# Moving bonus products, a bonus shuffle and two weight differences in a fused RWKV6 + SiLU kernel

## The chip, the cores and the metric

The kernel runs on one core of a Trainium2 chip. Its time is the device time of a launch in microseconds (us), given as the median of several runs. A profiled execution is one launch recorded by the hardware profiler; its span runs from the first to the last recorded instruction and is a little shorter than the launch's own time. The engines are TensorE (PE in the profile; its weight loads are PEld), VectorE (DVE), ScalarE (ACT), GpSimd (POOL) and SyncE (SP, which here issues the DMAs).

## The reference

All data are float32. Batch 4, 8 heads, 768 tokens, head dimension 48; then a two-layer network over the 3072 tokens.

```python
# rwkv6: r, k, v, w are (4, 8, 768, 48), u is (8, 48)
for t in range(S):
    kt, vt, rt, wt = k[:, :, t], v[:, :, t], r[:, :, t], w[:, :, t]
    cur = einsum('bhd,bhe->bhde', u * kt, vt)
    y[:, :, t] = einsum('bhd,bhde->bhe', rt, state + cur)
    state = wt[..., None] * state + einsum('bhd,bhe->bhde', kt, vt)
x = y.transpose(0, 2, 1, 3).reshape(3072, 384)
h = x @ w_in                        # 384 x 2048
out = (h * sigmoid(h)) @ w_out      # 2048 x 384
```

## The kernel before, in words

**Units.** The work is cut into 12 units: six chunks of 128 tokens, each for two pairs of batches. Unit i covers 2 batches x 8 heads x 128 tokens. Instead of stepping through tokens, a unit builds for each head a 128 x 128 matrix `score` of token against token, by levels: level l joins blocks of c = 2^l tokens. `score_products` (L687 on, its matmuls recorded as L698 or L706) makes a level's entries on TensorE, and they are copied under a mask into `score` (L716 for a whole level, L803 for a corner of one, or ACT copies at L796 where c is 32 or more). `grow_queries` (DVE, L621), `grow_keys` (POOL, L639) and `prepare` (DVE, L774) multiply the decays into queries and keys between levels. From unit 2 on two levels are made together: `burst(i, l)` makes levels l and l + 1. Then `y_values` multiplies `score` by the values, `update` moves the state on (L882 to L898), and the result goes to `xt`, the input of the network.

**Bonus.** The diagonal of `score` is the "bonus" r·(u k), and near neighbours are made with it. Units 0 and 1 do it for pairs of tokens on TensorE's side; units 2 and 3 for pairs of tokens on POOL and DVE:

- `load_rk(i)` has SP load r and k of the unit into `tokens_rk` (four transfers, L107).
- `bonus(i, x)` has three POOL products: x = 0 at L442, x = 1 at L444, x = 2 at L446 (times u).
- `bonus_sum(i, x)` has DVE reduce the products into `own_sums` (L451; two at L455), and behind the last of them four SP transfers bring the sums to their rows (`diag`).
- `bonus_spread(i)` has five ACT copies into `both_b` and a DVE shuffle (L589 to L592), and `bonus_write(i)` has two masked DVE copies into `score` (L598).

From unit 4 on the same is done for blocks of 8 tokens (`block_bonus` L501, `block_sum` L535, `block_move`, `block_spread` with ACT copies at L562/L564 and a shuffle at L565, `block_write` at L571). Unit 4 is NPAIR, unit 2 is NTOK; NL is 7 and FIRST is 3.

**The network.** `up(i, m)` makes two of the sixteen slices of h (L990, then the SiLU into `gt` on ACT, L999). For unit 0 `down` (L1012) multiplies plainly by `w_out_sb`. From unit 1 on the second product is made by seven products of half size (`quarter`, L1056) from sums and differences: `sums` on the gt side (DVE, L1038), `weight_sums` on the weight side (DVE, L1030, once for the whole kernel, four steps 0 to 3 that write into `own` and `w_out_sb`). The results are added up at L1065 (DVE).

**The weights.** w_in and w_out arrive in 16 pieces, loaded by SP (L206), and each is rounded before TensorE reads it: `head_weight` (ACT, L223 and L225), `tail_weight` (ACT, L231), `join_weight` (two DVE operations, L242 and L243), `add_weight` (POOL, L255), which writes `w_in_sb`, `w_out_sb` or `own`. Pieces 8 and later belong to w_out.

**The order.** It is written out by hand. `do(...)` calls the steps one by one, and each step puts its instructions at the end of its engines' streams; nothing reorders them later. An engine takes its stream strictly in that order. The first units have long `do` lists of their own; from unit 3 on `mix(i)` gives a list of groups for unit i, and `room` says how many steps of the network (of units i - 1 and i - 2) follow each group. Semaphores between engines are set by the framework from reads and writes of the tiles.

Around the change, the order before is: the scores of unit 1's last level, weight piece 8, `y` and `update` of unit 1, piece 9, then pieces 10 to 15 each with a few steps of `up`, `down` and of unit 2 (`others`), then unit 2's levels 2 to 6.

Of the kernel before, what the change touches and what calls it, by code (L numbers as in the profile page):

```python
# [8 lines left out]
F32 = mybir.dt.float32  # L9
# [29 lines left out]
def kernel(  # L39
# [11 lines left out]
    nc = tc.nc  # L51
# [3 lines left out]
    L = 128  # L55
# [378 lines left out]
    def bonus(i, x):  # L434


        engine = nc.gpsimd if i > 0 or x == 0 else nc.vector
        if x == 0:
            ruk[i] = tokens_rk[:, 1] if i < NTOK else pt.tile([128, H, 2, D], F32, name="ruk", bufs=1)

            ruk[i, 0] = tokens_rk[:, 0, :, 0] if i < NTOK else ruk[i][:, :, 0]
            engine.tensor_tensor(out=ruk[i, 0], in0=rk(i, 0)[:, :, 1], in1=rk(i, 1)[:, :, 0], op=ALU.mult)  # L442
        elif x == 1:
            engine.tensor_tensor(out=ruk[i], in0=rk(i, 0), in1=rk(i, 1), op=ALU.mult)  # L444
        else:
            engine.tensor_tensor(out=ruk[i], in0=ruk[i], in1=u_bc[:, :, None, :].to_broadcast([128, H, 2, D]), op=ALU.mult)  # L446
# [229 lines left out]
    def corner(l, x):  # L676

        return x % 2, x if x % 2 == 0 else (L >> l) - 1 - x
# [2 lines left out]

    def score_products(i, l, queries, sc):
        c, ni = 1 << l, L >> (l + 1)
        if i > 0 or l == NL - 1:
            for p in range(NP):
                for x in range(4 if c == 32 else 2):
                    for e in range(2):  # L687
                        rows = slice(PD * e, PD * e + D)
                        if c >= 32:
                            b, first = corner(l, x)  # L690
                            q = (p, 2 * NP - 1 - p)[b]
                            to, have = sc[e][x * c:(x + 1) * c, q, first // 2 * c:(first // 2 + 1) * c], queries[rows, q, (first + 1) * c:(first + 2) * c]
                        else:
                            apart = 2 * (NP - p) - 1
                            to = dims_of(sc[e][x * 64:(x + 1) * 64, p, :], 32 * x, [apart * L // 2 + 32 - 64 * x, 2], [1, 32])
                            have = dims_of(queries[rows, p, :], 64 * x + c, [apart * L + 64 - 128 * x, 2], [2 * c, 32 // c], [1, c])
                        m = 32 if c == 32 else 64
                        nc.tensor.matmul(to, lhsT=tk[i][rows, X[l % 2] + p, x * m:(x + 1) * m], rhs=have, start=True, stop=True)  # L698
            return

        for p in range(NP):
            for e in range(2):
                rows = slice(PD * e, PD * e + D)

                apart, r_p, s_p = 2 * (NP - p) - 1, queries[rows, p, :], sc[e][:, p, :]
                nc.tensor.matmul(bass.AP(tensor=s_p.tensor, offset=s_p.offset,  # L706
                                         ap=[s_p.ap[0], [apart * L // 2, 2], [1, L // 2]]),
                                 lhsT=tk[i][rows, X[l % 2] + p, :],
                                 rhs=bass.AP(tensor=r_p.tensor, offset=r_p.offset + c,
                                             ap=[r_p.ap[0], [apart * L, 2], [2 * c, ni], [1, c]]),  # L710
                                 start=True, stop=True)
# [75 lines left out]
    def keep_level(i, l):  # L787
        c = 1 << l
        for e in range(2):
            if c < 32 and (i > NTOK or l == FIRST):  # L790
                keep_masked(i, l, e, made[i, l])
                continue
            for x in range(4 if c == 32 else 2):
                if c >= 32:
                    b, first = corner(l, x)
                    nc.scalar.copy(  # L796
                        out=score[x * c:(x + 1) * c, i % NSC, e, b * NP:(b + 1) * NP, (first + 1) * c:(first + 2) * c],
                        in_=made[i, l][e][x * c:(x + 1) * c, b * NP:(b + 1) * NP, first // 2 * c:(first // 2 + 1) * c])
                    continue
                rows = slice(x * 64, (x + 1) * 64)  # L800
                for b in range(NB):
                    half, inner = (x, 1 - x)[b], [1, c]
                    nc.vector.copy_predicated(  # L803
                        out=dims_of(score[rows, i % NSC, e, b * NP, :], 64 * half + c, [L, NP], [2 * c, 32 // c], inner),
                        mask=dims_of(masks[l][rows, b], 32 * half, [0, NP], [c, 32 // c], inner),
                        data=dims_of(made[i, l][e][rows, b * NP, :], 32 * half, [L // 2, NP], [c, 32 // c], inner))

    def go_on(i, l):

# [118 lines left out]
    def mix(i):  # L928
# [15 lines left out]
        def start(j):  # L944
            return [*[(product, j, l) for l in range(1, NL)], (grow_own, j, 1)]

        end = [[*at(ahead, *bonus_steps(i + 1, 0, 1, 2, 3))],
               [*at(i < len(units) - NB, (turn_apart, i), (turn_k, i)), *at(ahead, *turns(i + 1))],
               [(y_state, i), *both(y_values, i), *both(update, i), *at(ahead, *start(i + 1)),
                *at(ahead, *sum_steps(i + 1, 0, 1), *bonus_steps(i + 1, 4, 5)), (move_x, i)]]  # L950
        if i < NPAIR:
            groups = [[*both(turn, i, "w"), (product, i, 0)],
                      [*both(turn, i, "k"), *both(turn, i, "r"), (odd_ones, i)], [(start_levels, i), (prepare_keys, i, 1)],
                      [(prepare, i, 1), *[(product, i, l) for l in range(1, NL)]],
                      [(burst, i, 1), (keep_level, i, 1)],
                      [(keep_level, i, 2), (go_on, i, 2)],
                      [(prepare, i, 3), (reverse_v, i), (bonus, i, 0)],
                      [(burst, i, 3), (keep_level, i, 3), (bonus_sum, i, 0), (bonus, i, 1), (bonus, i, 2)],
                      [(keep_level, i, 4), (go_on, i, 4), (bonus_sum, i, 1), (load_rk, i + 1), (load_u,)],
                      [(prepare, i, 5), (make_block_mask,), (bonus_spread, i), (bonus_write, i)],  # L960
                      [(burst, i, 5), (keep_level, i, 5), (keep_level, i, 6), (go_on, i, 6)], *end]
        else:
            groups = [[], [(odd_keys, i, 2), (grow_keys, i, 2, False), (grow_queries, i, 2), *sum_steps(i, 2)],
                      [(prepare, i, 3), *bonus_steps(i, 6, 7)],
                      [(burst, i, 3), (keep_level, i, 3), *sum_steps(i, 3, 4), (block_move, i), *at(ahead, (load_rk, i + 1))],
                      [(keep_level, i, 4), (go_on, i, 4)],
                      [(prepare, i, 5), (reverse_v, i)],
                      [(block_spread, i), (block_write, i)],
                      [(burst, i, 5), (keep_level, i, 5), (keep_level, i, 6), (go_on, i, 6)], *end]

        loads = block_loads(i + NSLOT) if i + NSLOT < len(units) else []
# [153 lines left out]
    for m in range(1, 4):  # L1125
# [1 line left out]
    do((head_weight, 8), (join_weight, 7), (scores, 1, 5), (grow_keys, 1, 6), (add_weight,), (tail_weight, 8), (up, 0, 6),  # L1127
       (bonus_write, 1))

    do((scores, 1, NL - 1), (join_weight, 8), (add_weight,), (up, 0, 7), *both(y, 1), (turn_apart, 1),  # L1130
       (tail_weight, 9), (turn_k, 1), (dense_x, 1, 0), (head_weight, 9, [0]), (dense_x, 1, 1), (head_weight, 9, [1]),
       (join_weight, 9), (add_weight,), (tail_weight, 10), (head_weight, 10), *both(update, 1), (up, 1, 0), *both(turn, 2, "w"))
    blocks = block_loads(3)

    others = {0: [(up, 1, 1), (down, 0, 0, 0), *both(turn, 2, "k"), (product, 2, 0), (product, 2, 1)],
# [4 lines left out]
    for m in range(6):  # L1140
# [2 lines left out]
    second.append(ctx.enter_context(tc.tile_pool(name="po", bufs=1, space=bass.MemoryType.PSUM)))  # L1143

    blocks = block_loads(4)
    do(*blocks[0:2], (level, 2, 2), (prepare, 2, 3), (weight_sums, 1), (down, 0, 1, 0), (down, 0, 0, 3), (down, 0, 1, 1),
       (sums, 1, 0), (bonus, 2, 0), (bonus_sum, 2, 0))
    do(blocks[2], (burst, 2, 3), (keep_level, 2, 3), (keep_level, 2, 4), (go_on, 2, 4), (prepare, 2, 5), (bonus, 2, 1),
       (bonus, 2, 2), (down, 0, 1, 2), (bonus_sum, 2, 1), (load_rk, 3), (sums, 1, 1), *blocks[3:7], (down, 0, 1, 3))
    do((burst, 2, 5), (keep_level, 2, 5), (keep_level, 2, 6), (go_on, 2, 6), (up, 1, 6), (bonus_spread, 2), (bonus_write, 2),  # L1150
       (load_values, 3), (turn_apart, 2), (turn_k, 2), (up, 1, 7), (sums, 1, 2))
    do((sums, 1, 3), (y_state, 2), *both(y_values, 2), *both(update, 2),
       (move_x, 2),
       *blocks[7:])
# [1 line left out]
    for i in range(3, len(units)):  # L1156
        steps = downs(i - 2) + ups(i - 1)
        groups = mix(i)
        if i == NTOK + 1:

            groups[2].append((weight_sums, 2))
            groups[4].insert(1, (weight_sums, 3))
        room = (1, 1, 0, 2, 1, 1, 1, 1, 1, 2, 2, 1, 1, 0) if i < NPAIR else (3, 2, 2, 1, 1, 1, 2, 1, 1, 1, 0)
        for group, count in zip(groups, room):
            do(*group)
            for step in steps[:count]:
                do(*step)
            steps = steps[count:]
# [32 lines left out]
```

## Time and profile before

| what | value |
|---|---|
| median of 3 runs | 612.73 us (612.69 to 615.25) |
| profiled execution, its own time | 611.3 us |
| span of the profiled execution | 609.5 us, granted TensorE clock 0.997 |
| PE busy | 594.1 us, 97% of the span |
| DVE, POOL, ACT busy | 423.8, 367.2, 232.7 us (70%, 60%, 38%) |
| L990 (first product of the network), 1152 matmuls | 258.9 us, 382 ns each |
| L255 `add_weight` | 1.82 us each |
| L242 and L243 `join_weight` | 0.96 and 0.95 us |
| L442, L444, L446 bonus products of a pair unit | 1.18, 1.81, 1.80 us |
| L1030 `weight_sums` | 1.75 and 2.22 us |
| unit 2: burst of levels 1, 3, 5 starts at | 88.59, 105.74, 113.82 us |

Times in the timeline are microseconds from the start of the span. A row of the timeline gives the start, the duration, the engine, the line, the operation with its output and inputs, and how many instructions were put together; behind it in brackets stands the idle time of the engine ahead of that row and what ended it. A wait that is given to an engine is the one that ended last by the profile.

### The profile page before, as it was taken

The page shows a single profiled execution, that of the slowest core. Times are in us where ns is not written, and L with a number is a line of the kernel's source. Part 1 is how long each engine was busy: PE and PEld are TensorE (multiplying, and loading weights), DVE is VectorE, ACT ScalarE, POOL GpSimd, SP SyncE. Part 2 cuts the span into 40 slices and gives each one's busy share as a digit, 9 for nine tenths or more (in the row PEclk, how much of TensorE's full clock was granted, in tenths as well). Part 3 has the DMA queues.
Part 4 walks back from the last instruction along what each step waited for, and adds up shares of the span by engine and source line. Part 5 has one row for each costly group of instructions (what it writes and reads, how often), then busy time and mean ns, then how long its engine had stood idle before and what let it go on. Part 6 is the DMA issues. An engine that isn't in the chain of part 4 may idle for free.

```text
span 609.5 us, 15190 instructions
## 1 busy us (share of the span) xinstructions
PE 594.1 (97%) x5998; PEld 530.7 (87%) x5998; DVE 423.8 (70%) x715; ACT 232.7 (38%) x516; POOL 367.2 (60%) x414
## 2 busy tenths in 40 slices
PE   8999999899999997999999999999999999999997
PEld 7778876699889897889889889989989989989997
DVE  7879779898795495587588587487587597561041
ACT  6799792431530440351351252242252242241110
POOL 6998488557667278378468578568568658500000
PEclk9999999999999998999999999999999999999999
DMA  9966774353543643643543552552452312100000
GB/s 222 300 164 169 147 232 49 72 98 48 128 62 53 135 61 53 129 65 52 121 70 53 113 80 51 108 89 50 97 95 48 81 44 53 36 3 27 26 1 26
DMA packets 203079, 53.44 MB, mean 88 GB/s; under 512 B 186752, under 2 KB 194816, under 8 KB 203008
## 3 DMA queue, kind: packets, MB, share of 16 engines
q1 hardware_dynamic: 201424, 51.88, 41.6%
q8 instruction: 47, 0.77, 0.6%
q10 hardware_dynamic: 1584, 0.59, 0.4%
q14 instruction: 24, 0.20, 0.1%
HBM read 43.21 MB, written 5.24 MB: 79 GB/s over the span
## 4 chain that ended last, share of the span: by engine, by line
PE 72%; DVE 12%; DMA 4%; POOL 3%; ACT 3%; issue 3%; SPq 3%; DVEq 0%; POOLq 0%; ACTq 0%
PE p_h L990 31%; PE p_o L1056 30%; PE p_m L855 2%; DVE score L716 2%; DVE temps L1038 2%; DVE tr L621 2%; SPq L123 2%; PE p_sc L698 2%; POOL tk L639 2%; PE p_m L698 1%; DMA raw<-in_w_dram 1%; PE p_m L847 1%; DMA tokens_w<-in_w_dram 1%; DVE p_w L242 1%; DMA raw<-in_r_dram 1%
## 5 line engine op out<-in xcount | busy, mean ns | idle before, releaser
L990 PE MATMUL p_h<-xt,w_in_sb 128*128 128x256 f32 x1152 | 258.9, 382 | 1.8 <-POOL w_in_sb L255 1.1
L990 PEld LDWEIGHTS p_h<-xt,w_in_sb 128*128 128x128 f32 x1152 | 215.9, 190 | 32.8 <-POOL w_in_sb L255 1.2
L999 ACT ACTIVATE gt<-p_h 128x512 f32<-128x512 f32 x90 | 53.3, 596 | 189.2 <-PE p_h L990 188.8
L639 POOL TENSOR_TENSOR tk<-tk,tw 128x256 f32<-128x256 f32 x128 | 93.7, 753 | 43.5 <-issue 22.9
L1056 PE MATMUL p_o<-own,temps 128*128 128x192 f32 x528 | 90.2, 331 | 4.5 <-DVE temps L1065 4.5
L1056 PEld LDWEIGHTS p_o<-own,temps 128*128 128x128 f32 x528 | 87.6, 193 | 5.4 <-DVE temps L1065 5.3
L1056 PE MATMUL p_o<-w_out_sb,gt 128*128 128x192 f32 x508 | 87.4, 328 | 0.0
L1056 PEld LDWEIGHTS p_o<-w_out_sb,gt 128*128 128x128 f32 x508 | 82.7, 190 | 0.9 <-issue 0.4
L501 POOL TENSOR_TENSOR ruk<-tokens_rk 128x768 f32<-128x768 f32 (+1 forms) x32 | 50.0, 1573 | 52.0 <-DMA tokens_rk<-in_k_dram 31.9
L1038 DVE TENSOR_TENSOR temps<-gt 128x256 f32<-128x256 f32 x84 | 56.9, 677 | 22.4 <-ACT gt L999 22.4
L621 DVE TENSOR_TENSOR tr<-tr,tw 128x512 f32<-128x512 f32 x61 | 56.4, 924 | 15.3 <-PE p_m L698 12.4
L422 POOL TENSOR_TENSOR tw<-tw 128x256 f32<-128x256 f32 (+6 forms) x83 | 43.3, 521 | 36.4 <-DVE tw L374 32.5
L609 ACT COPY tk<-tk 128x256 f32<-128x256 f32 x52 | 20.9, 403 | 99.0 <-POOL tk L639 71.7
L1065 DVE TENSOR_TENSOR partial<-p_o,partial 128x192 f32<-128x192 f32 x33 | 11.8, 358 | 38.9 <-PE p_o L1056 38.7
L1038 DVE TENSOR_TENSOR temps<-temps,gt 128x256 f32<-128x256 f32 x43 | 32.1, 748 | 1.5
L716 DVE COPY_PREDICATED score<-mask,p_sc 128x512 f32<-128x512 int8 x42 | 31.1, 795 | 2.7 <-PE p_sc L698 2.5
L1056 PE MATMUL p_o<-w_out_sb,temps 128*128 128x192 f32 x176 | 30.4, 326 | 0.0
L1065 DVE TENSOR_TENSOR temps<-p_o,partial 128x192 f32<-128x192 f32 x22 | 7.9, 357 | 31.9 <-PE p_o L1056 22.4
L860 ACT COPY yt<-p_m 48x512 f32<-48x512 f32 x40 | 23.2, 581 | 14.9 <-PE p_m L855 8.7
L1056 PEld LDWEIGHTS p_o<-w_out_sb,temps 128*128 128x128 f32 x176 | 28.9, 190 | 0.0
L698 PEld LDWEIGHTS p_sc<-tr,tk 48*32 48x32 f32 (+1 forms) x1312 | 18.1, 119 | 11.6 <-issue 6.3
L501 POOL TENSOR_TENSOR spare<-tokens_rk 128x384 f32<-128x384 f32 (+1 forms) x16 | 28.1, 1754 | 0.0
(180 smaller groups left out, 845.7 us busy)
## 6 DMA issues: line engine op xcount, KB each, us to landing
w_out_sb<-in_moe_w_in_dram SPq DMA_DIRECT2D x6, 768.0 KB, 7.5
w_out_sb<-in_moe_w_out_dram SPq DMA_DIRECT2D x4, 768.0 KB, 5.2
own<-in_moe_w_out_dram SPq DMA_DIRECT2D x4, 768.0 KB, 5.9
tokens_rk<-in_r_dram SPq DMA_DIRECT2D x8, 384.0 KB, 4.4
tokens_rk<-in_k_dram SPq DMA_DIRECT2D x8, 384.0 KB, 5.3
tokens_w<-in_w_dram SPq DMA_DIRECT2D x8, 384.0 KB, 6.5
xt<-yt SPq DMA_DIRECT2D x60, 48.0 KB, 2.0
raw<-in_w_dram SPq DMA_DIRECT2D x80, 32.0 KB, 2.4
```

The source lines that it names most:

```text
L422: engine.tensor_tensor(out=up, in0=t[:, :, 0::2], in1=t[:, :, 1::2], op=ALU.mult)
L501: mul = lambda out, one, two: nc.gpsimd.tensor_tensor(out=out, in0=one, in1=two, op=ALU.mult)
L609: nc.scalar.copy(out=keys(i, X[(l + 1) % 2] * L + c, [4 * c, blocks], [c, 2], [1, c]), in_=keys(i, NP * L + c, [4 * c, blocks], [NP * L + ...
L621: nc.vector.tensor_tensor(out=odd, in0=odd, in1=tw[i][l][:, :, 0::2][:, :, :, None].to_broadcast([128, Q, L >> (l + 1), c]), op=ALU.mult)
L639: nc.gpsimd.tensor_tensor(out=out, in0=have, in1=odd_products(i, l, b, *blocks), op=ALU.mult)
L698: nc.tensor.matmul(to, lhsT=tk[i][rows, X[l % 2] + p, x * m:(x + 1) * m], rhs=have, start=True, stop=True)
L716: nc.vector.copy_predicated(out=dst, mask=masks[l][:, :, None].to_broadcast([128, NB, NP, ni, c]), data=sc[e].rearrange("p (b q) (i c) -> ...
L860: nc.scalar.copy(out=yt[i][PD * e:PD * e + D, :, b, :], in_=p_yt[i, e][PD * b:PD * b + D])
L990: nc.tensor.matmul(p_h[:, a, :], lhsT=w_in_sb[:, c, f * 128:(f + 1) * 128], rhs=xt[i][:, c, :], start=(c == 0), stop=(c == KC - 1))
L999: nc.scalar.activation(out=gt[i, m], in_=p_h, func=AF.Silu)
L1038: nc.vector.tensor_tensor(out=out, in0=one, in1=two, op=op)
L1056: nc.tensor.matmul(p, lhsT=left(f), rhs=right[:, f, :], start=(f == 0), stop=(f == FH - 1))
```

## The change

Five edits, all in the order of the steps or in the form of one step:

1. Unit 2's three bonus products and their sums are issued right behind the scores of unit 1's last level, among weight pieces 8 and 9, instead of among unit 2's own levels 2 to 5. Their results go into the tiles `spare` and `partial` instead of a tile `ruk`. The load of unit 3's r and k goes with them.
2. `bonus_spread(2)` is issued ahead of unit 2's burst of levels 5 and 6, and `bonus_write(2)` ahead of `up(1, 6)`.
3. `weight_sums(1)` and `weight_sums(2)` are issued behind unit 2's burst of levels 5 and 6 (before: ahead of `down(0, 1, 0)`, and in unit 3's third group).
4. Unit 2's level 4 uses the full form of `score_products` and of the masked copy, as level 3 does.
5. Unit 4's `block_spread` and `block_write` are issued behind its levels 5 and 6 instead of ahead of them.

```diff
         if x == 0:
-            ruk[i] = tokens_rk[:, 1] if i < NTOK else pt.tile([128, H, 2, D], F32, name="ruk", bufs=1)
+            if i == NTOK:
+                free = pt.tile([128, 4, DM // 2], F32, name="partial", bufs=1)
+                ruk[i] = free.rearrange("p x d -> p (x d)").rearrange("p (h s d) -> p h s d", h=H, s=2)
+            else:
+                ruk[i] = tokens_rk[:, 1] if i < NTOK else pt.tile([128, H, 2, D], F32, name="ruk", bufs=1)
...
+            if i == NTOK:
+                ruk[i, 0] = spare[:, 0:H * D].rearrange("p (h d) -> p h d", h=H)
...
-        if i > 0 or l == NL - 1:
+        if (i > 0 or l == NL - 1) and (i, l) != (NTOK, FIRST + 1):
...
-            if c < 32 and (i > NTOK or l == FIRST):
+            if c < 32:
                 keep_masked(i, l, e, made[i, l])
                 continue
...
-        end = [[*at(ahead, *bonus_steps(i + 1, 0, 1, 2, 3))],
+        end = [[*at(i == NPAIR, (block_spread, i), (block_write, i)), *at(ahead, *bonus_steps(i + 1, 0, 1, 2, 3))],
...
-                      [(block_spread, i), (block_write, i)],
+                      [*at(i > NPAIR, (block_spread, i), (block_write, i))],
...
-    do((scores, 1, NL - 1), (join_weight, 8), (add_weight,), (up, 0, 7), *both(y, 1), (turn_apart, 1),
+    do((scores, 1, NL - 1), (bonus, 2, 0), (bonus, 2, 1), (join_weight, 8), (add_weight,), (bonus_sum, 2, 0), (bonus, 2, 2), (up, 0, 7), *both(y, 1), (turn_apart, 1),
        (tail_weight, 9), (turn_k, 1), (dense_x, 1, 0), (head_weight, 9, [0]), (dense_x, 1, 1), (head_weight, 9, [1]),
-       (join_weight, 9), (add_weight,), (tail_weight, 10), (head_weight, 10), *both(update, 1), (up, 1, 0), *both(turn, 2, "w"))
+       (join_weight, 9), (add_weight,), (tail_weight, 10), (head_weight, 10), *both(update, 1), (bonus_sum, 2, 1), (load_rk, 3), (up, 1, 0), *both(turn, 2, "w"))
...
-    do(*blocks[0:2], (level, 2, 2), (prepare, 2, 3), (weight_sums, 1), (down, 0, 1, 0), (down, 0, 0, 3), (down, 0, 1, 1),
-       (sums, 1, 0), (bonus, 2, 0), (bonus_sum, 2, 0))
-    do(blocks[2], (burst, 2, 3), (keep_level, 2, 3), (keep_level, 2, 4), (go_on, 2, 4), (prepare, 2, 5), (bonus, 2, 1),
-       (bonus, 2, 2), (down, 0, 1, 2), (bonus_sum, 2, 1), (load_rk, 3), (sums, 1, 1), *blocks[3:7], (down, 0, 1, 3))
-    do((burst, 2, 5), (keep_level, 2, 5), (keep_level, 2, 6), (go_on, 2, 6), (up, 1, 6), (bonus_spread, 2), (bonus_write, 2),
-       (load_values, 3), (turn_apart, 2), (turn_k, 2), (up, 1, 7), (sums, 1, 2))
+    do(*blocks[0:2], (level, 2, 2), (prepare, 2, 3), (down, 0, 1, 0), (down, 0, 0, 3), (down, 0, 1, 1), (sums, 1, 0))
+    do(blocks[2], (burst, 2, 3), (keep_level, 2, 3), (keep_level, 2, 4), (go_on, 2, 4), (prepare, 2, 5), (down, 0, 1, 2),
+       (bonus_spread, 2), (sums, 1, 1), *blocks[3:7], (down, 0, 1, 3))
+    do((burst, 2, 5), (keep_level, 2, 5), (keep_level, 2, 6), (go_on, 2, 6), (bonus_write, 2), (up, 1, 6), (weight_sums, 1),
+       (load_values, 3), (turn_apart, 2), (turn_k, 2), (up, 1, 7), (weight_sums, 2), (sums, 1, 2))
...
-            groups[2].append((weight_sums, 2))
```

More of the change, by code (lines that the diff above doesn't have):

```diff
@@ L789, in keep_level @@
         for e in range(2):
-            if c < 32 and (i > NTOK or l == FIRST):
+            if c < 32:
                 keep_masked(i, l, e, made[i, l])
                 continue
[L793 to L806, printed above, removed]
+            for x in range(L // c):
+                b, first = corner(l, x)
+                nc.scalar.copy(
+                    out=score[x * c:(x + 1) * c, i % NSC, e, b * NP:(b + 1) * NP, (first + 1) * c:(first + 2) * c],
+                    in_=made[i, l][e][x * c:(x + 1) * c, b * NP:(b + 1) * NP, first // 2 * c:(first // 2 + 1) * c])
     def go_on(i, l):
```

## The prediction

> **What bounds the kernel now.** I read the page first: engines, the chain that ended last, TensorE's waits. Then I went through the two stretches that the change touches (60 to 140 us, 200 to 240 us) engine by engine. The chain, and the complete list of TensorE's waits for other engines between 60 and 240 us (columns: engine, tile, line, releaser; us in total, times, longest):
>
> ```profile
> PE 72%; DVE 12%; DMA 4%; POOL 3%; ACT 3%; issue 3%; SPq 3%; DVEq 0%; POOLq 0%; ACTq 0%
> ```
> ```profile
> PE p_o L1056 <- DVE temps L1065: 4.5, 2, 3.3
> PE p_sc L698 <- DVE tr L621: 1.6, 1, 1.6
> PE p_h L990 <- POOL w_in_sb L255: 1.1, 1, 1.1
> PE p_m L698 <- POOL tk L639: 0.9, 1, 0.9
> PE p_o L698 <- DVE tr L774: 0.3, 1, 0.3
> ```
>
> TensorE is the bound: 97% busy, and here it waits 8.4 us in all. Work that the change takes from DVE, POOL or ACT pays only through one of these rows; work that it makes late costs as soon as TensorE needs the result. From 65 to 110 us TensorE is busy 5.00 of every 5.00 us, so there is no pause to absorb a delay.
>
> TensorE's timeline (start, duration, count, idle before and releaser) places what matters:
>
> ```profile
> 78.16 2.74 PE L1012 MATMUL p_m<-w_out_sb,own 128*128 128x384 f32 x8
> ...
> 88.59 0.70 PE L698 MATMUL p_sc<-tr,tk 48*64 48x64 f32 x32
> ...
> 113.82 0.75 PE L698 MATMUL p_sc<-tr,tk 48*32 48x32 f32 x64 [1.56 <-DVE tr L621]
> ...
> 137.54 0.69 PE L698 MATMUL p_m<-tr,tk 48*64 48x64 f32 x32 [0.95 <-POOL tk L639]
> ...
> 183.41 5.47 PE L1056 MATMUL p_o<-own,temps 128*128 128x192 f32 x32 [1.22 <-DVE temps L1065]
> ...
> 233.43 7.15 PE L1056 MATMUL p_o<-own,temps 128*128 128x192 f32 x32 [3.33 <-DVE temps L1065]
> ```
>
> At 78.16 the first down product of unit 0 starts on w_out_sb. 88.59 is burst(2,1), 113.82 burst(2,5), 137.54 burst(3,2). The next two views decide the forecast: SP's DMAs, then POOL's instructions, around the place where unit 2's bonus products are to go.
>
> ```profile
> 66.93 1.30 SPq L107 DMA_DIRECT2D tokens_rk<-in_r_dram  x2
> 68.33 1.27 SPq L107 DMA_DIRECT2D tokens_rk<-in_k_dram  x2
> ```
> ```profile
> DMA to landing us min/median/max: 6.4/6.4/6.6
> ```
> ```profile
> 67.30 1.81 POOL L255 TENSOR_TENSOR w_out_sb<-temps 128x768 uint32<-128x768 uint32 x1 [3.52 <-issue]
> 73.52 1.83 POOL L255 TENSOR_TENSOR w_out_sb<-temps 128x768 uint32<-128x768 uint32 x1 [4.41 <-ACT temps L225]
> 77.69 1.82 POOL L255 TENSOR_TENSOR w_out_sb<-temps 128x768 uint32<-128x768 uint32 x1 [2.34 <-ACT temps L223]
> ```
>
> Unit 2's r and k are issued between 66.9 and 69.6; the last starts at 69.0 and lands 6.4 us later, at **75.4**. The POOL rows are add_weight for pieces 8, 9, 10. Pieces 8 and 9 end at 69.1 and 75.35, only 9.1 and 2.8 us before the matmuls at 78.16 need them.
>
> **What the Trainium skill says.** "Perfetto Trace Analysis", "DMA Instruction — HWDGE (DVE, Sync)": the profiled DMA row ends when the sequencer is done; the data movement comes later. The trace agrees: 0.6 us per issue, 6.4 us to landing. "TensorE: Matmul & The Clock Gate", architectural detail: ACT, DVE and GpSimd queues are strict FIFO. So an instruction that waits at the head holds all behind it; no row before disagrees. Same page, "What's actually happening": an idle window of about 3.4 us halves the clock. After the 3.33 us gap at 233, 32 matmuls take 7.15 us, 5.47 in the row of 183: agrees, worth 1.7 us. "SBUF — State Buffer", "SBUF: two separate sides": a DVE operation with two SBUF inputs and a GpSimd one exclude each other. L1038 takes 0.42 us alone and 1.92 or 2.03 while POOL works: agrees.
>
> **Part 1, bonus products of unit 2.** Before, POOL's three (1.18, 1.81, 1.80 us) and DVE's three sums (3 x 0.54) ran at 105 to 115 us. Now POOL's order is add 7, bonus 0, bonus 1, add 8, bonus 2, add 9; DVE's is join 8, sum, join 9, state copies, two sums, transposes, join 10. All wait in order for the landing at 75.4.
> POOL: bonus 0 ends 76.65, bonus 1 78.5, add 8 80.3 (was 69.1), bonus 2 82.15, add 9 84.0 (was 75.35). TensorE reaches the down product at 78.16: it waits 2.2 us for piece 8, runs two matmuls, waits 2.4 us for piece 9. That alone is 4.6 us.
> DVE: sum 77.25, join 9 79.25 (a pair takes 2.0), state copies 80.4, two sums behind bonus 2 83.25, transposes of w 84.5, join 10 86.5 where it was 77.5. The weight chain goes on from there, each step behind the one before on its engine: add 10 (1.82) 88.35; on DVE a transpose pair (1.3) and join 11 (2.0) 89.75, on POOL two L422 (1.73) and add 11 91.95; transposes and join 12 93.0, five L422 (2.06) and add 12 95.8; unit 2's start_keys (L663, 1.30) 97.1. TensorE, already 4.6 late, meets them in order: up(1,2) 85.4 to 88.1, 0.3 us for piece 10, 2.3 for piece 11, and 1.45 ahead of burst(2,1), since start_keys stands behind add 12. The sum 4.6 + 0.3 + 2.3 + 1.45 is **+8.7 us**: burst(2,1) near 97.3, not 88.59. The floor is 4.6, if the chain of 10 to 12 catches up. Behind it TensorE is full again: burst(2,2) near 105.9, burst(2,3) near 114.4.
> SP: four diag transfers and the four issues of load_rk(3), some 0.6 us each, move ahead of the `own` loads of pieces 14 and 15 (77.62); they wait for the sums at 83.25, so those loads go out near 88 and land 5.9 later, about 94. Piece 14 was joined at 89.94 and will be near 98: nothing. load_rk(3) waits for bonus 2 (82.15), which frees its room; its reader comes after 130: nothing. The rooms `spare` and `partial` have no other user until up(1,3) and unit 1's quarters: nothing.
>
> **Part 2, what leaves the stages of 97 to 121 us.** Ahead of burst(2,5) DVE loses weight_sums(1) (2.22), the first sum (0.54), 8 corner copies (2.03) for 2 full ones (2 x 0.65), and contention in the 2.32 us L621 (1.0 alone): 4.8 us, against a gap of 1.56: **-1.56**. What would be late next is L774, 0.3, also behind the same chain. The full form on TensorE takes 1.16 us instead of 0.69: **+0.45**. ACT's both_b copies no longer wait for diag (DVE idles 2.26 us at 118.3 for them), off TensorE's path: 0, between 0 and -0.3.
>
> **Part 3, weight_sums 1 and 2** go to DVE behind burst(2,5); their users are unit 1's quarters, from 138 us, at least 15 us later: 0. From ahead of burst(3,2), 2.2 us and its lock against POOL disappear: the gap 0.95 goes, **-0.95** (none, if POOL's L639 is late for itself).
>
> **Part 4, unit 4's shuffle** goes behind level 6. DVE no longer idles 8.03 us for ACT's `spare` (at 209.13), so the sums start after L621. But L621 itself waits for the burst of level 6, which ends at 209.55: of the 2.65 us of shuffle and L571, 2.2 are won there. Then the shuffle waits in order on ACT, whose copies now stand behind 12 score copies and a silu: 214.65; two L571 (2.5) end 217.45, the last sums 219.9, the next transposes start as before (219.95 for 220.03). The gaps of 183 and 233 stay: **0**, between -6.25 (3.33 + 1.22 + 1.7 of clock) and +2.5, should the copies lie later.
>
> Sum: 8.7 - 1.56 + 0.45 - 0.95 = +6.6 on the profiled 611.3 (span 609.5): 617.9. The median of the runs, 612.73, lies 1.4 above; I take 612.73 + 6.3, **619.0**, since the catch-up of pieces 10 to 12 is likelier partial than nil.
>
> **Rivals.** (A) *Faster.* The wait on unit 2's loads isn't felt and the clock drop at 233 goes: -1.56 - 0.95 + 0.45 - 3.33 - 1.7 = -7.1, 605.6; with the gap of 183 too, 604.4. It decides at the landing: add 9 ends landing + 8.5, and TensorE needs it at 79.5, so r and k must be there by 71.0. For it: add 8 alone would have 9 us of slack. Against: the landing is 75.4 and SP's queue ahead of it is unchanged. Chance 0.07. (B) *Near no change.* The delay stands, but unit 4's move removes both gaps and the clock drop: +6.6 - 6.25, about 613.1. Against: the place of the copies on ACT. Chance 0.06. (C) *Slower still.* The new gaps between 78 and 97 us, 4.6 us idle within 6, lower the clock: +1.7 to +3.4, 621 to 622.5. For: 3.33 us sufficed at 233; against: two pieces with matmuls between. Chance 0.18. (D) *Catch-up.* Only the floor: +4.6 - 2.06 = +2.5, 615.2, inside what a measurement can tell. For: the durations of the chain are those of rows that overlapped other work; against: every link above is in order on one engine. Chance 0.09. My forecast has the remaining 0.60.
>
> **How the numbers follow.** Low end 614.5 takes in D; high end 622.5 takes in C; A and B are left out, 0.13, and some of the ends. About 0.5% (3.06 us) is what a measurement of this kernel can tell from no change: faster is under 609.7 (A, 0.07), within it B and D (0.15), slower over 615.8 my forecast and C (0.78).
>
> **What would show it.** Right: bonus 0 on POOL shows some 9 to 12 us of idle time released by DMA tokens_rk, TensorE's down product at 78 waits for POOL w_out_sb (L255) over 4 us, burst(2,1) starts near 97.3, no gap ahead of burst(2,5), the gaps of 183 and 233 still there some 7 us later. Wrong: r and k land before 71; burst(2,1) under 92; or no clock below 0.9 between 235 and 250.

## The result and the profile after

The changed kernel takes **618.93 us** (median of 6 runs, 617.5 to 621.25) where the kernel before takes 612.5 (6 runs, 610.88 to 615.25). The ratio is 1.012, with a 95% interval of 1.0095 to 1.0145: slower by some 6 to 9 us. The forecast was 619.0. The profiled execution took 619.96 us, its span is 618.2 us. One execution each of E1 and E6 took twice the usual time and one of E7 was more than 1.5% above that kernel's fastest; the medians and ratios below leave these three out.

The lines of the changed kernel are 6 higher than before for the steps from the bonus products to `prepare` (L448 is L442, L627 is L621, L704 is L698) and 3 lower from `turn_k` on (L1009 is L1012, L1053 is L1056). E4, E5 and E8 have the same numbers; in E2 and E10 all of these lines are 6 higher than before (L1018, L1062), and in E9 L1055 and L1064 are L1053 and L1062 of the changed kernel.

The chain that ended last, and the complete list of TensorE's waits between 60 and 250 us (engine, tile, line, releaser; us in total, times, longest):

```profile
PE 78%; DVE 7%; POOL 5%; DMA 4%; SPq 3%; issue 2%; ACT 1%; POOLq 0%; DVEq 0%; ACTq 0%
```
```profile
PE p_m L1009 <- POOL w_out_sb L255: 6.7, 4, 2.5
PE p_o L1053 <- DVE temps L1062: 4.5, 2, 3.3
PE p_h L987 <- POOL w_in_sb L255: 1.1, 1, 1.1
PE p_o L1053 <- DVE temps L1035: 0.6, 1, 0.6
```

A new first row stands there, four waits for `w_out_sb`, released by add_weight on POOL. The waits for L621, L774 and L639 of before are gone. A row of 0.6 us has come in at L1053. TensorE's timeline of the changed kernel shows where these waits lie:

```profile
80.70 1.56 PE L1009 MATMUL p_m<-w_out_sb,own 128*128 128x384 f32 x4 [2.52 <-POOL w_out_sb L255]
84.25 1.56 PE L1009 MATMUL p_m<-w_out_sb,own 128*128 128x384 f32 x4 [1.99 <-POOL w_out_sb L255]
...
88.68 1.56 PE L1009 MATMUL p_m<-w_out_sb,own 128*128 128x384 f32 x4 [0.29 <-POOL w_out_sb L255]
92.15 2.16 PE L1009 MATMUL p_m<-w_out_sb,gt 128*128 128x384 f32 x4 [1.91 <-POOL w_out_sb L255]
94.10 3.89 PE L987 MATMUL p_h<-xt,w_in_sb 128*128 128x256 f32 x12
97.92 0.70 PE L704 MATMUL p_sc<-tr,tk 48*64 48x64 f32 x32
...
122.14 0.76 PE L704 MATMUL p_sc<-tr,tk 48*32 48x32 f32 x64
...
190.53 5.47 PE L1053 MATMUL p_o<-own,temps 128*128 128x192 f32 x32 [1.22 <-DVE temps L1062]
...
237.11 0.92 PE L1053 MATMUL p_o<-own,temps 128*128 128x192 f32 x4 [0.60 <-DVE temps L1035]
241.36 8.02 PE L1053 MATMUL p_o<-own,temps 128*128 128x192 f32 x32 [3.33 <-DVE temps L1062]
```

POOL's timeline, and the landing of unit 2's r and k (issued between 67.44 and 70.1), show what released them:

```profile
76.10 1.00 POOL L448 TENSOR_TENSOR spare<-tokens_rk 128x384 f32<-128x384 f32 x1 [12.47 <-DMA tokens_rk<-in_k_dram]
...
78.83 1.82 POOL L255 TENSOR_TENSOR w_out_sb<-temps 128x768 uint32<-128x768 uint32 x1
...
82.38 1.82 POOL L255 TENSOR_TENSOR w_out_sb<-temps 128x768 uint32<-128x768 uint32 x1
...
95.94 1.29 POOL L669 TENSOR_TENSOR tk<-tk,tw 128x128 f32<-128x128 f32 x2
```
```profile
DMA to landing us min/median/max: 6.3/6.3/6.5
```

POOL stands idle for 12.47 us until the last of the four transfers is there. Adds 8 and 9 follow at 78.83 and 82.38, where they had been done at 69.1 and 75.35. The last row is unit 2's start_keys, on which burst(2,1) waits; it ends at 97.23.

### The profile page after: what moved, and what is told of

The parts are those of the page before. It is cut to its first block, busy times and chain, and to the rows that moved or that the text cites. A ratio compares the mean times of both kernels' runs of the same rounds, so it can differ in the third digit from the quotient of the medians.

```text
span 618.2 us, 15148 instructions
## 1 busy us (share of the span) xinstructions
PE 598.1 (97%) x5982; PEld 532.6 (86%) x5982; DVE 414.3 (67%) x709; ACT 232.6 (38%) x516; POOL 366.3 (59%) x414
## 4 chain that ended last, share of the span: by engine, by line
PE 78%; DVE 7%; POOL 5%; DMA 4%; SPq 3%; issue 2%; ACT 1%; POOLq 0%; DVEq 0%; ACTq 0%
PE p_h L987 35%; PE p_o L1053 31%; PE p_m L1009 3%; PE p_m L852 2%; PE p_sc L704 2%; SPq L123 2%; PE p_m L704 2%; POOL tk L645 1%; PE p_m L844 1%; DMA tokens_w<-in_w_dram 1%; POOL w_in_sb L255 1%; DVE p_w L242 1%; DMA tokens_rk<-in_k_dram 1%; DVE tr L627 1%; DVE score L722 1%
## 5 line engine op out<-in xcount | busy, mean ns | idle before, releaser
L645 POOL TENSOR_TENSOR tk<-tk,tw 128x256 f32<-128x256 f32 x128 | 90.8, 730 | 48.2 <-issue 22.9
L1053 PE MATMUL p_o<-own,temps 128*128 128x192 f32 x528 | 91.5, 333 | 5.2 <-DVE temps L1062 4.5
L1053 PEld LDWEIGHTS p_o<-own,temps 128*128 128x128 f32 x528 | 88.5, 195 | 6.4 <-DVE temps L1062 5.4
L1053 PE MATMUL p_o<-w_out_sb,gt 128*128 128x192 f32 x508 | 87.4, 328 | 0.0
L1053 PEld LDWEIGHTS p_o<-w_out_sb,gt 128*128 128x128 f32 x508 | 82.7, 190 | 0.9 <-issue 0.4
L627 DVE TENSOR_TENSOR tr<-tr,tw 128x512 f32<-128x512 f32 x61 | 55.7, 913 | 26.4 <-PE p_m L704 22.7
L1035 DVE TENSOR_TENSOR temps<-gt 128x256 f32<-128x256 f32 x84 | 52.9, 630 | 22.4 <-ACT gt L996 22.4
L1062 DVE TENSOR_TENSOR partial<-p_o,partial 128x192 f32<-128x192 f32 x33 | 11.8, 358 | 41.0 <-PE p_o L1053 40.9
L1035 DVE TENSOR_TENSOR temps<-temps,gt 128x256 f32<-128x256 f32 x43 | 30.4, 706 | 1.5
L1053 PE MATMUL p_o<-w_out_sb,temps 128*128 128x192 f32 x176 | 30.4, 326 | 0.0
L1062 DVE TENSOR_TENSOR temps<-p_o,partial 128x192 f32<-128x192 f32 x22 | 7.9, 357 | 32.5 <-PE p_o L1053 23.0
L1053 PEld LDWEIGHTS p_o<-w_out_sb,temps 128*128 128x128 f32 x176 | 28.9, 190 | 0.0
L884 POOL TENSOR_TENSOR state<-state,tw 128x512 f32<-128x512 f32 x16 | 21.9, 1389 | 10.3 <-PE p_m L844 10.3
```

The lines of the kernel that those rows point to most:

```text
L627: nc.vector.tensor_tensor(out=odd, in0=odd, in1=tw[i][l][:, :, 0::2][:, :, :, None].to_broadcast([128, Q, L >> (l + 1), c]), op=ALU.mult)
L645: nc.gpsimd.tensor_tensor(out=out, in0=have, in1=odd_products(i, l, b, *blocks), op=ALU.mult)
L884: nc.gpsimd.tensor_tensor(out=new, in0=new, in1=tw[i][NL][:, b * NP:(b + 1) * NP, :].to_broadcast([128, NP, 2 * PD]), op=ALU.mult)
L1035: nc.vector.tensor_tensor(out=out, in0=one, in1=two, op=op)
L1053: nc.tensor.matmul(p, lhsT=left(f), rhs=right[:, f, :], start=(f == 0), stop=(f == FH - 1))
```

## The experiments

The ratios are those of each kernel to the kernel before, run on the same chip, with 95% intervals. The kernel before took 611.3 to 611.6 us there (medians).

**E1. The products back, the rest of the change kept.**

```diff
-    do((scores, 1, NL - 1), (bonus, 2, 0), (bonus, 2, 1), (join_weight, 8), (add_weight,), (bonus_sum, 2, 0), (bonus, 2, 2), (up, 0, 7), ...
+    do((scores, 1, NL - 1), (join_weight, 8), (add_weight,), (up, 0, 7), ...
...
-       (join_weight, 9), ..., *both(update, 1), (bonus_sum, 2, 1), (load_rk, 3), (up, 1, 0), *both(turn, 2, "w"))
+       (join_weight, 9), ..., *both(update, 1), (up, 1, 0), *both(turn, 2, "w"))
```

Products, sums, load_rk(3), bonus_spread, bonus_write and the tile `ruk` are where they were before (the edits of `bonus` and of unit 2's later steps aren't shown here).

> The whole change without its first part: unit 2's products, sums, load_rk(3) and bonus_spread where they were before. Theory (the loss is the wait in order for unit 2's r and k, handed on by the weight chain; unit 4's move costs 1.5): burst(2,1) back at 88.6, no gap ahead of burst(2,5), 612.5 - 1.56 - 0.95 + 0.45 + 1.5 = 611.9 us. Rival (unit 4's move and the clock drops around it make the loss): still some 3 us or more above the kernel before, 615.5 and up.

Measured: 617.99 us, ratio 1.010 (1.0075 to 1.0125). **A miss for my theory**, and a case for another one: undoing the first part takes away nearly none of the loss. The only trace of this kernel has a span of 1223.8 us and can't be compared with the others; E6 and E7 have the same steps at this place.

**E2. The products' move alone.** The kernel before with the first part of the change only.

> The first part alone, on the kernel before: products, their sums and load_rk(3) among pieces 8 and 9; weight differences, level 4 and unit 4 as before. Theory: POOL idle 12 us for the landing of unit 2's k, TensorE's four waits for w_out_sb of 6.7 us and a slow clock behind them, burst(2,1) at 97.9; the 1.56 us gap ahead of burst(2,5) shrinks, since the sums and POOL's products have left that stage: 612.5 + 9.3 - 1.0 = 620.8 us. Rival (unit 4): not over 616.

Measured: 616.87 us, ratio 1.0091 (1.0067 to 1.0115), 4 us under what I expected. TensorE's timeline:

```profile
91.81 1.56 PE L1018 MATMUL p_m<-w_out_sb,gt 128*128 128x384 f32 x4 [1.91 <-POOL w_out_sb L255]
...
96.98 0.70 PE L704 MATMUL p_sc<-tr,tk 48*64 48x64 f32 x32 [1.02 <-POOL tk L669]
...
120.58 0.76 PE L704 MATMUL p_sc<-tr,tk 48*32 48x32 f32 x64
```

The waits for `w_out_sb` are there again (6.1 us in four), burst(2,1) is 8.4 us late, and behind it there is no slow clock. At burst(2,5) the delay is only 120.58 - 113.82 = 6.8: the gap of 1.56 us has gone whole, although weight_sums(1) and the eight corner copies are still in that stage. So the leaving of the products is enough to close this gap; the two other edits weren't needed for it. E6 shows further down that these two are enough as well.

**E3. Unit 4's move alone.**

```diff
-        end = [[*at(ahead, *bonus_steps(i + 1, 0, 1, 2, 3))],
+        end = [[*at(i == NPAIR, (block_spread, i), (block_write, i)), *at(ahead, *bonus_steps(i + 1, 0, 1, 2, 3))],
...
-                      [(block_spread, i), (block_write, i)],
+                      [*at(i > NPAIR, (block_spread, i), (block_write, i))],
```

> Unit 4's block_spread and block_write behind its level 6, on the kernel before, nothing else. Theory after the result: the two L571 meet POOL's products of unit 5 (3.9 us in place of 2.5), the last sums end 0.8 us late, a second gap of 0.6 us opens ahead of the one of 3.33, and the clock falls to half: +1.5 us, 614.0. The prediction on record: 0. Rival: the slow clock behind it is chance, and the move itself gives some -0.5 to +0.5.

Measured: 614.74 us, ratio 1.0055 (1.0033 to 1.0077): +2.0 to +4.7 us, so the move costs. TensorE's timeline shows a wait for L1038 that the kernel before hasn't, and the known gap unchanged:

```profile
231.78 0.92 PE L1056 MATMUL p_o<-own,temps 128*128 128x192 f32 x4 [0.98 <-DVE temps L1038]
236.02 7.15 PE L1056 MATMUL p_o<-own,temps 128*128 128x192 f32 x32 [3.33 <-DVE temps L1065]
```

The second row stands 2.6 us later than before (233.43), but 1.4 of this was there at unit 4's burst of level 5 (209.65, before 208.25), ahead of the edit; some 1.2 us are the edit's in this trace. Much of the rest goes with the clock. Each run has a mean granted clock, and span x (1 - clock) estimates what a slow clock cost it: 3.3 us on average in E3 and 1.7 in the kernel before on the same chip. The two parts make 2.8 us, and the medians are 3.1 apart. None of E3's 7 runs has a clock above 0.997, while 7 of the 20 of the kernel before have 0.999 or more. Why the move brings the slow clock more often isn't shown.

**E4. The whole change, unit 2's r and k loaded earlier.**

```diff
-    others = {1: blocks[8:12], 2: [(bonus_sum, 1, 0), (bonus_sum, 1, 1), (load_rk, 2), *both(update, 0)],
+    others = {1: [], 2: [(bonus_sum, 1, 0), (bonus_sum, 1, 1), (load_rk, 2), *blocks[8:12], *both(update, 0)],
```

> The whole change, with one more edit: the load of unit 2's r and k is issued ahead of the sixteen loads of raw r (12 us earlier on SP), so that it lands near 63 us. Theory (what is lost is the wait for the landing): POOL's first product starts near 64 with no wait for a DMA, adds 8 and 9 end by 69 and 75.5, TensorE has no wait for w_out_sb, burst(2,1) at 88.6: 612 us, the same as with the products back in their old place. Rival (what is lost is the 4.8 us of POOL and 1.5 us of DVE work put into a full weight chain): burst(2,1) still 4 to 6 us late, 616 to 618 us.

Measured: 612.25 us, ratio 1.0005 (0.999 to 1.002). One reordered load takes back the loss. POOL's timeline and TensorE's first late matmul:

```profile
68.46 1.01 POOL L448 TENSOR_TENSOR spare<-tokens_rk 128x384 f32<-128x384 f32 x1 [4.16 <-DMA tokens_rk<-in_k_dram]
...
74.77 1.83 POOL L255 TENSOR_TENSOR w_out_sb<-temps 128x768 uint32<-128x768 uint32 x1
```
```profile
90.91 0.70 PE L704 MATMUL p_sc<-tr,tk 48*64 48x64 f32 x32 [1.73 <-POOL tk L669]
```

I had the landing at 63; it is 68.4, because SP took 5.2 us for the four issues (2.7 in the kernel before) and the transfers took up to 9.2. POOL still waits 4.16 us. But add 9 ends at 76.6, ahead of the need near 80, and TensorE has no wait for `w_out_sb`. That fits the bound of the prediction, r and k by 71.0. The gap of 1.73 us at burst(2,1) is what is left for the rival: POOL's 4.6 us of products are in the weight chain, whenever the data come. It isn't a fixed price: with the same work and the same load ahead of it, the gap is 0.33 us in E8, 0.72 in E9 and 1.36 in E10.

**E5. The same work in the weight chain, but behind piece 9.** The products are issued behind add 9, the sums and load_rk(3) behind `up(1, 2)`; the rest is the change.

```diff
-       (join_weight, 9), ..., *both(update, 1), (bonus_sum, 2, 1), (load_rk, 3), (up, 1, 0), ...
+       (join_weight, 9), ..., (bonus, 2, 0), (bonus, 2, 1), (bonus, 2, 2), *both(update, 1), (up, 1, 0), ...
...
-              1: [(up, 1, 2), *both(turn, 2, "r"), ...
+              1: [(up, 1, 2), (bonus_sum, 2, 0), (bonus_sum, 2, 1), (load_rk, 3), *both(turn, 2, "r"), ...
```

> The whole change with POOL's three products of unit 2 behind add 9 instead of around add 8, and DVE's sums and load_rk(3) behind join 11: the same work in the weight chain, but at a place where its data have landed (75.4). Theory (the wait for the landing is most of the loss): pieces 8 and 9 in time; 4.8 us of POOL work less the idle 2.3 ahead of add 10 push the adds 10 to 12 and start_keys, so burst(2,1) is 2 to 3 us late: 613.5 to 615. Rival (where the products stand among the pieces doesn't matter): 617 to 619 as with the whole change.

Measured: 613.21 us, ratio 1.0032 (1.0017 to 1.0046), 0.3 us under the range that I expected. POOL waits 1.47 us for the landing. burst(2,1) is at 92.68, 4.1 us late and more than I had, with a slow clock ahead of it. One wait of 1.91 us for `w_out_sb` is left, where there were four of 6.7:

```profile
86.91 2.44 PE L1009 MATMUL p_m<-w_out_sb,gt 128*128 128x384 f32 x4 [1.91 <-POOL w_out_sb L255]
```

**E6. Weight differences and level 4 alone; E7. the weight differences alone.** Both on the kernel before, the differences behind bonus_write(2) as in the change; E7 leaves out level 4's full form. The diff shows the differences alone; weight_sums(2) also leaves unit 3's third group.

```diff
-    do(*blocks[0:2], (level, 2, 2), (prepare, 2, 3), (weight_sums, 1), (down, 0, 1, 0), ...
+    do(*blocks[0:2], (level, 2, 2), (prepare, 2, 3), (down, 0, 1, 0), ...
...
-    do((burst, 2, 5), ..., (up, 1, 6), (bonus_spread, 2), (bonus_write, 2),
-       (load_values, 3), (turn_apart, 2), (turn_k, 2), (up, 1, 7), (sums, 1, 2))
+    do((burst, 2, 5), ..., (up, 1, 6), (bonus_spread, 2), (bonus_write, 2), (weight_sums, 1),
+       (load_values, 3), (turn_apart, 2), (turn_k, 2), (up, 1, 7), (weight_sums, 2), (sums, 1, 2))
```

> Weight differences 1 and 2 behind bonus_write(2) and unit 2's level 4 in the full form, on the kernel before; products and unit 4 as before. The prediction on record gave these parts -2.1. Theory after the run with the products back (618): with the sums of the bonus late, bonus_write(2) waits for diag and for ACT, the two differences (3.5 us on DVE) now stand behind it, and sums(1, 2) and (1, 3) come too late for unit 1's quarters: TensorE waits at L1056 near 135 us for DVE, then a slow clock; 615 us. Rival (what was slow there was unit 4's move): 610 to 611.

> Weight differences 1 and 2 behind bonus_write(2), on the kernel before, nothing else. Theory (the differences are what makes DVE late): the same wait at L1056 near 135 us as with both parts, 615 us less some 0.5 for level 4's longer matmuls. Rival (the full form of level 4 is the cause): 611 us, no such wait.

Measured: E6 613.71 us, ratio 1.0042 (1.0022 to 1.0061); E7 613.02 us, 1.0028 (1.0009 to 1.0048). The edits to which the prediction gave -2.1 **cost** 1.7 to 2.6 us by the ratios when they stand alone. DVE's timeline of E6, then TensorE's:

```profile
120.81 0.01 DVE L592 LOAD_MASK_SELECT both_b<-both_b  x1 [2.58 <-ACT both_b L591]
...
121.02 2.50 DVE L598 COPY_PREDICATED score<-own_mask,both_b 128x1024 f32<-128x1024 int8 x2
123.42 2.58 DVE L1021 TENSOR_TENSOR own<-w_out_sb,own 128x1536 f32<-128x1536 f32 x1
...
136.20 0.36 DVE L1056 TENSOR_TENSOR temps<-p_o,partial 128x192 f32<-128x192 f32 x1
```
```profile
113.82 0.76 PE L698 MATMUL p_sc<-tr,tk 48*32 48x32 f32 x64
...
130.61 2.76 PE L1047 MATMUL p_o<-own,temps 128*128 128x192 f32 x16
136.61 4.55 PE L1047 MATMUL p_o<-own,temps 128*128 128x192 f32 x16 [3.24 <-DVE temps L1056]
```

(L1021, L1047 and L1056 of this kernel are L1030, L1056 and L1065 before.) With the products in their old place DVE still stands 2.58 us for `both_b`; behind it now stand two differences of 2.6 us each, and the add of unit 1's quarter (L1056) comes at 136.2, so that TensorE waits 3.24 us and then takes 4.55 us for 16 matmuls that take 2.76 at full clock: 5.0 us lost. On the other side the gap of 1.56 us ahead of burst(2,5) is gone here too (the row at 113.82 has none), with the products in their old place, and so is that of 0.95 ahead of burst(3,2). E6 accounts for E1 by the times: E1 is E6 with unit 4's move, and 1.0042 and 1.0055 make 1.0097, measured 1.010. That E1 has the same wait isn't shown. In the whole change this wait doesn't come. The shuffle for `both_b` is done at 120.7, ahead of the burst, bonus_write(2) ends 6.2 us behind the burst's start (9.7 in E6), and the two differences take 1.75 us each: they run for the most part ahead of POOL's product of the state (L884, from 130.82), where in E6 the same product (L878, 122.72 to 126.90) runs beside them.

**E8. The change with the earlier load and without unit 4's move.**

> The whole change with the load of unit 2's r and k ahead of raw r, and without unit 4's move. Theory (the loss is the wait for the landing plus 1.5 to 3 us of unit 4's move): 612.25 - 2.3 = 610 us, just below the kernel before, with 1.7 us left at burst(2,1) and no wait ahead of burst(2,5) and of burst(3,2). Rival (unit 4's move costs nothing here): 612, no difference from the run with the move.

Measured: 609.24 us, ratio 0.9967 (0.9951 to 0.9983), faster than the kernel before. E4 differs in unit 4's move alone, and takes 3.0 us more by the medians, 2.3 by the ratios.

**E9. E8, with the quarter's adds ahead of unit 4's and 5's first sums.** grow_own(1), block_sum 0 and 1 and block_bonus 4 and 5 go from the end of the unit before to the second group of their own, behind three quarters (`late` is the list of these steps; where E8 differs from the change isn't shown):

```diff
+        late = lambda j: [(grow_own, j, 1), *sum_steps(j, 0, 1), *bonus_steps(j, 4, 5)]
...
-            return [*[(product, j, l) for l in range(1, NL)], (grow_own, j, 1)]
+            return [(product, j, l) for l in range(1, NL)]
...
-                *at(ahead, *sum_steps(i + 1, 0, 1), *bonus_steps(i + 1, 4, 5)), (move_x, i)]]
+                *at(ahead and i not in (3, 4), *late(i + 1)), (move_x, i)]]
...
-            groups = [[], [(odd_keys, i, 2), ...
+            groups = [[], [*at(i in (4, 5), *late(i)), (odd_keys, i, 2), ...
```

> The change with the earlier load and without unit 4's move, and one more edit: units 4 and 5 issue grow_own(1), block_sum 0 and 1 and block_bonus 4 and 5 behind the first three quarters of the unit two before, so that DVE makes the quarter's adds (L1062) ahead of the sums (0.94 + 0.54 us) and of one L627 (0.8 us). Theory (the stalls near 183 and 231 are only DVE's order, and the slow clock follows from the length of the second): the gap of 2.9 us falls to about 1, the 1.3 one to 0, and the row behind takes 5.5 us instead of 8.4: 609.2 - 1.9 - 1.3 - 2.9 = 603 us; ratio 0.987. Rival (the unit's later levels become late instead, so that TensorE waits at a burst near 200 and 250): no gain, 609.

Measured: 606.87 us, ratio 0.9935 (0.9909 to 0.9961): the fastest here, some 4 us under the kernel before, though 4 us over my expectation. By the ratios the edit itself brings some 2 us over E8, a third of the 6 that I had, and the two intervals just overlap. TensorE's timeline of E8, then of E9, at the same step:

```profile
231.20 8.39 PE L1053 MATMUL p_o<-own,temps 128*128 128x192 f32 x32 [2.92 <-DVE temps L1062]
```
```profile
229.38 5.47 PE L1055 MATMUL p_o<-own,temps 128*128 128x192 f32 x32 [1.20 <-DVE temps L1064]
```

The gap shrinks from 2.92 to 1.20 us, and the 32 matmuls behind it run at full clock; 5 of E9's 6 runs have a mean clock of 0.999 or more, 10 of 22 in E8. The wait near 182 is gone as well. What eats into the expected gain are waits that weren't there: two for the next adds (0.6 us at 186.7, 0.2 at 235.0) and one of 1.4 us for L1064 at 277.9, a unit later.

**E10. The products' move alone, with the earlier load.**

> The products' move alone (weight differences, level 4 and unit 4 as in the kernel before), with the load of unit 2's r and k ahead of raw r. Theory (taking the products out of the stage ahead of burst(2,5) is what closes its gap, and the differences and level 4 add little once they have gone): burst(2,1) 0.3 to 1.7 us late, no gap ahead of burst(2,5), the 0.9 us gap ahead of burst(3,2) still there: 611.3 - 1.56 + 0.8 = 610.5. Rival (the differences' move does it): 612, with a gap of 1 us or more ahead of burst(2,5).

Measured: 609.79 us, ratio 0.9976 (0.9959 to 0.9993). No gap ahead of burst(2,5), 1.36 us ahead of burst(2,1), 0.59 ahead of burst(3,2). Against E8 the differences and level 4 in the full form bring at most about a microsecond, which these intervals don't resolve.

## Why the prediction was right, and where it was not

**The wait for the loads: right, in size and mechanism.** Against the steps of Part 1:

| step | predicted | in the profile after |
|---|---|---|
| POOL idle for the landing | 9 to 12 us | 12.47 us |
| adds 8 and 9 end | 80.3, 84.0 | 80.65, 84.2 |
| TensorE's waits for pieces 8, 9, 10, 11 | 2.2, 2.4, 0.3, 2.3 | 2.52, 1.99, 0.29, 1.91 |
| gap ahead of burst(2,1) | 1.45 | none; slow clock, 1.74 |
| burst(2,1) starts | 97.3 | 97.92 |

The last step but one came out through another term. The rows of 92.15 and 94.10 take 2.16 and 3.89 us where 1.56 and 2.75 are usual; start_keys was done meanwhile. It ends at 97.23, where I had 97.1, so the slow clock stands for the most part in the place of the wait and adds 0.6 us: a small share of rival C. E2 shows the same step without a slow clock, with a wait of 1.02 us and burst(2,1) at 96.98. Between the waits for pieces 8 and 9 stand four matmuls, not two. E4 shows the cause alone: only the loads come earlier, and the ratio goes from 1.012 to 1.0005. E5 has the same work in the chain, with 1.47 us of waiting for the data: 1.0032. The Trainium skill, "TensorE: Matmul & The Clock Gate", architectural detail, has the GpSimd queue as strict FIFO (first in, first out); the trace agrees, with POOL idle for 12.47 us ahead of an add whose inputs had been ready since 67 us.

**Part 2: the sum right, with more ground than it needed.** The gap of 1.56 us is gone and level 4 takes 1.16 us instead of 0.69, as worked out. But I listed four things that leave the stage, 4.8 us against 1.56, and didn't ask which suffices. E2 and E10 show that the products' leaving does, and E6 that the differences and level 4 do without it. So this part can't be counted for the products' move alone, nor for the other two edits.

**Part 3: the zero was conditional.** The gap of 0.95 us ahead of burst(3,2) is gone, as worked out. "At least 15 us later: 0" held in the whole change and failed in E6 and E7. I counted the distance from the differences to their users in time and not the work that stands between on DVE, nor that bonus_write(2) ahead of them waits for ACT while the products are late, nor that they themselves become longer beside POOL's product of the state.

**Part 4: the mis-sized term.** I kept 2.5 us for the two masked copies at their new place. The copies and POOL's first product of unit 5 before, then DVE's timeline of the changed kernel and POOL's beside it:

```profile
209.39 2.50 DVE L571 COPY_PREDICATED score<-spare 128x1024 f32<-128x1024 int8 x2
```
```profile
212.38 2.08 POOL L501 TENSOR_TENSOR ruk<-tokens_rk 128x768 f32<-128x768 f32 x1 [9.58 <-DMA tokens_rk<-in_k_dram]
```
```profile
221.61 0.01 DVE L571 LOAD_MASK_SELECT spare<-spare  x1 [2.55 <-ACT spare L570]
...
221.86 3.91 DVE L577 COPY_PREDICATED score<-spare 128x1024 f32<-128x1024 int8 x2
```
```profile
222.57 2.03 POOL L507 TENSOR_TENSOR spare<-tokens_rk 128x384 f32<-128x384 f32 x1
224.68 1.92 POOL L507 TENSOR_TENSOR tokens_rk<-tokens_rk,tokens_w 128x384 f32<-128x384 f32 x1
```

They take 3.91 us: before, they ran ahead of POOL's products of unit 5, and now they run into them. I had named the lock between DVE and GpSimd (the Trainium skill, "SBUF — State Buffer", "SBUF: two separate sides") for L1038 and not applied it to this row, whose mask and data both lie in SBUF. The traces agree with it: beside POOL's products the copies take 3.91, 4.25 (E3) and 3.86 us (E4), ahead of them 2.50 (before and E8). From there the sums end 0.8 us late against the rest, and a gap of 0.60 opens ahead of 237.11. The shift grows from 7.1 us at 190.53 to 8.8 at 249.21: +1.7 in place of 0, inside the bound of +2.5. About half of this is the new gap and what follows from it. The other half is the row behind the 3.33 us gap, which takes 8.02 us instead of 7.15, and that isn't shown to be the move's: the same row takes 7.15 us in E3, with the move, and 8.39 in E8, without it. By time alone the move costs 2.0 to 4.7 us (E3) and 2.3 to 3.0 (E4 against E8), more than any one trace shows. That a slow clock would come in more runs was no term of the prediction.

**The sum.** The profiled execution is 8.7 us longer, not 6.6: I had 0.6 too little at burst(2,1), and nothing for the 1.7 between 190 and 249 us. The medians are 6.4 us apart, because the profiled execution of before lies 1.2 us under its kernel's median of 612.5 and the one after 1.0 above its own. I had taken 6.3 as the step between the medians for a catch-up of pieces 10 to 12, and no catch-up is seen. So the closeness of 619.0 to 618.93 is partly luck; the range from 614.5 to 622.5 is what the working supported.

## What to carry to other kernels

Before an instruction is moved ahead in a stream that is taken in order, look up when its data land, not when their load was issued, and compare that with the first result that someone needs from the instructions behind it. Here one view (SP's issues and their time to landing) and one subtraction (71.0 against 75.4) told the loss, and issuing that load 10 us earlier took a loss of 1.2% back to nothing (E4). Edits that "cost nothing" must be tested for what else is in the change: the weight differences were free in the whole change, where another part had taken away the wait ahead of them, and not by themselves.

## What the runs showed of the hardware

The length of a pause alone doesn't tell whether TensorE's clock falls behind it. In these traces, between 60 and 300 us, rows behind gaps of up to 1.73 us run at full speed. Behind longer gaps both happen. The gaps of 2.52 and 1.99 us of the changed kernel are followed by 1.56 us for four matmuls, the usual time. The same gap of 1.91 us is followed by 1.56 us in E2, by 2.16 in the changed kernel and by 2.44 in E5. The 32 matmuls behind the gap of 3.33 us take 7.15 us before and in E3, 7.67 in E5 and 8.02 in the changed kernel, but 5.47 in E6, where it ends at 237.61; and they take 7.15 us in E7 behind a gap of only 2.14. The granted clock behind E5's gap of 1.91 us (which ends at 86.91), then around E6's of 3.33 (columns: stretch, its length, then busy time and instructions of TensorE, its weight loads, DVE, ACT and POOL, and after them the clock, the share of the DMA engines and GB/s):

```profile
86.00:88.00 2.00, 1.09 (x3) 0.66 (x4) 1.67 (x3) 1.51 (x3) 1.84 (x3) 0.86 1.01 257
88.00:90.00 2.00, 2.00 (x6) 1.22 (x5) 1.29 (x2) 1.95 (x3) 1.84 (x4) 0.50 0.78 176
90.00:92.00 2.00, 2.00 (x9) 1.69 (x8) 1.13 (x3) 1.37 (x2) 2.00 (x4) 0.79 0.65 106
```
```profile
235.00:240.00 5.00, 2.39 (x15) 2.40 (x16) 4.06 (x10) 0.41 (x1) 3.43 (x5) 1.00 0.23 59
240.00:245.00 5.00, 5.00 (x32) 5.00 (x32) 2.41 (x6) 0.92 (x2) 4.92 (x8) 1.00 0.26 46
```

Runs of one kernel differ in the same way. Of the 119 runs of the kernel before that stand beside the experiments, 32 have a mean clock of 0.999 or 1.0 and take 610.0 us on average, 58 have 0.996 or 0.997 (611.4 us), and 29 have 0.994 or less (612.7 us). None of the 54 runs with unit 4's move (the changed kernel, E1, E3, E4 and E5) has a clock above 0.997, while 10 of 22 have in E8, which is E4 without the move. So one trace doesn't price a pause: for an order of work, the pauses of under 1.8 us were harmless to the clock in all of these traces, and a longer one added up to 2.9 us behind itself (E8), or nothing (E6).
